# Softmax attention and a Fourier layer on one core: v loaded whole or in quarters

## The chip, the core and the metric

The kernel runs on 1 core of one Trainium2 chip. The core has five engines that each execute their own instructions in order: TensorE (PE, matmuls; its weight loads are shown as PEld), VectorE (DVE), ScalarE (ACT), GpSimd (POOL) and SyncE (SP), which here issues all DMA transfers. The time is the device time of one execution in microseconds (us); lower is better. Before the change it is 3046.23 us, the median of 3 runs (3045.86 to 3047.76).

## What is computed

Two independent layers, whose outputs stand side by side in the result. All data are 32-bit floats.

```
A:  x [1, 2048, 1024], wqkv [1024, 3072], wo [1024, 1024], 32 heads of 32 columns
    q, k, v = split(x @ wqkv)
    p = softmax(q k^T / sqrt(32))          per head, 2048 x 2048
    a = (p v, heads joined) @ wo
B:  x [1, 2048, 1024], DFT matrices of 2048 and of 1024, real and imaginary
    a = x dft_hid_re^T,  b = x dft_hid_im^T
    y = dft_seq_re a - dft_seq_im b
out = concat(A, B) in the last axis
```

## The kernel before

**Stages.** The large products (x with wqkv, the two DFT products, the projection with wo) are done in blocks with seven products in place of eight, and each 32-bit operand is split into a high and a low half, so that three matmuls (high by high, low by high, high by low) make one. These matmuls have line L356, whatever product they belong to. Their operands are loaded (L404, L413), added or subtracted (L420) and split: the high half at L442 (VectorE) or L440 (ScalarE), the low half at L445 (GpSimd or VectorE). The results of the first product, q, k and v, are stored to DRAM: `qk_d` and `v_d`. `v_d` consists of two tensors of 128 rows by 16 key tiles by 512 columns, so each holds v for 16 heads.

**Attention.** It runs head by head, with the matmuls of L356 of the other stages put between as fill. Per head there are three streams on PE:

- S, L1147: scores with the query in the rows, 128 x 1024 at a time, into one of two banks of `psS`. VectorE takes the negated row maxima (L1153), ScalarE the exponentials with the row sums (L1156), which gives the bank free.
- T, L1264: the scores transposed, 128 keys by 512 queries, into one of two banks of `psT`. The row maximum is already part of the product, by two more rows of `qs` (loaded at L1194). ScalarE writes the exponentials to one of 19 tiles `pt` (L1268).
- V, L1282: after every four key tiles (`PVB` = 4), 16 products of v with `pt` are added up in `pd`, with the four blocks of 512 queries in four column groups of the array. VectorE adds `pd` to `ot` (L1293, L1295). So a head has four groups of V, and group number t // 4 uses key tiles t-3 to t of v.

At the end `ot` is multiplied by the reciprocal row sums `rt` (loaded at L1228, four transfers) and stored (L1312).

**Loads for attention.** q and k of head h + 2 (`qs`, `ks`, L280) and v of head h + 2 (`vt`, two buffers, L1247) are asked for when head h is done with its buffers. v of a head is one transfer: 128 partitions, 16 key tiles, 32 columns, so 128 x 16 runs of 128 bytes, 256 KB.

**What sets the order.** The order of the instructions on all engines is made by a planner (class `Plan`) when the program is built. Every piece of work is an `Op` with an engine, an assumed cost, the ops that it waits for (`after`), a rank (the lowest goes first) and, for a DMA, its size `kb`. The planner goes through an assumed time. A DMA keeps SP for `ISSUE` = 0.46 us, the DMA stretch for kb / 360 us, and it has landed `LANDING` = 1.6 us later; SP begins none while more than 1 us of DMA work is outstanding or the eighth last hasn't landed. Fill is taken on PE when no stream is able, and in proportion to the progress of attention. Loads for fill have the number of finished groups as rank, the loads of attention have -2, those of L1194 -3. The real program has this order on each engine, and semaphores for the true dependences; the assumed times are not in it.

In the load of v, `vt_r.take()` returns the ops that used the buffer last (`old`) and a list for its new users; `v_st` holds the stores of `v_d`; `att_gate` what has to be done before the first buffers of attention exist:

```
vts[h] = (op("SP", ISSUE, load, old + v_st[h // 16] + (att_gate if h < 2 else []), [users], -2, 512), users)
```

The 512 is the size in KB that the planner counts, twice the real 256.

Of the kernel before, what the change touches and what calls it, by code (L numbers as in the profile page):

```python
# [8 lines left out]
F32 = mybir.dt.float32  # L9
# [7 lines left out]
P = 128  # L17
# [3 lines left out]
DH = 32  # L21
NC = D // P
NS = S // P
# [3 lines left out]
PVB = 4  # L27
# [33 lines left out]
class Plan:  # L61
# [23 lines left out]
    def op(self, engine, cost, emit, after=(), uses=(), rank=0.0, kb=0, order=None, other=None, lanes=1, two=False):  # L85

        o = Op(engine, cost, emit, rank, kb, other, two)
        o.lanes = lanes  # L90
        seen = set()
        for d in after:
            if d is not None and id(d) not in seen:
                seen.add(id(d))
                self._wait(o, d)
        for u in uses:
            u.append(o)
        if order is not None:
            p, order.first = order.first, o
            if p is not None and not p.begun:  # L100
                p.soon.append(o)
                o.left += 1
        if o.left == 0:
            self._release(o)
        return o
# [104 lines left out]
def kernel(  # L210
# [11 lines left out]
    nc = tc.nc  # L222
# [6 lines left out]
    v_d = [dram.tile([P, NS, NB], F32, name=f"v_d{b}") for b in range(2)]  # L229
# [17 lines left out]
    def f(ap):  # L247
        return ap.bitcast(F32)
# [43 lines left out]
    def att():  # L292

        if "att" not in late:
            vp.release()
            late["att"] = a = tc.alloc_tile_pool(name="att", bufs=1, reuse_waits="tile")
            QS.append(a.tile([98, S], F32R, name="qs1"))
            KS.append(a.tile([98, S], F32R, name="ks1"))
            nc.gpsimd.memset(f(KS[1])[96:98, :], 1.0)
        return late["att"]  # L300
# [3 lines left out]
    MM, PV, SWITCH, TINY = 0.234, 0.762, 0.62, 0.17  # L304
# [3 lines left out]
    ISSUE = 0.46  # L308
# [16 lines left out]
    op = pl.op  # L325
# [204 lines left out]
    v_st = [[], []]  # L530
    att_gate = []
# [586 lines left out]
    def load_qk_op(h, which, j, after):  # L1118
        g = h // 4
        got[h, which, j] = op("SP", ISSUE, lambda: load_qk(h, which, j), [*qk_st[2 * g + which][j], *after], [], -2, 192)  # L1120
# [118 lines left out]
    VT = {}  # L1239
    vts = {}  # L1240

    def load_v(h):
        old, users = vt_r.take()

        def load():
            VT[h] = att().tile([P, NS, DH], F32, name="vt", bufs=2)
            nc.sync.dma_start(VT[h], v_d[h // 16][:, :, h % 16 * DH : h % 16 * DH + DH])  # L1247

        vts[h] = (op("SP", ISSUE, load, old + v_st[h // 16] + (att_gate if h < 2 else []), [users], -2, 512), users)

    def transposed(h):
        moved = mine[h][4]
        todo = []
        po = {}
        oold, ouse = ot_r.take()
        for t in range(NS):
            for j in range(4):
                old, users = psT_r.take()
                pold, puse = pt_r.take()
                box = {}  # L1260

                def mm(t=t, j=j, box=box):
                    box["p"] = psT.tile([P, NB], F32, name="psT")
                    nc.tensor.matmul(box["p"], KS[h % 2][0:98, t * P : t * P + P], QS[h % 2][0:98, j * NB : j * NB + NB], start=True, stop=True)  # L1264

                def ex(box=box):
                    box["t"] = att().tile([P, NB], F32, name="pt", bufs=NPT)
                    nc.scalar.activation(box["t"], box["p"], AF.Exp)  # L1268

                a = op("PE", MM, mm, [*old, *moved, *(att_gate if h == t == j == 0 else []), *(got.get((h, w, k)) for w, k in ((0, j), (1, t // 4)))], [users])  # L1270
                e = op("ACT", ET, ex, [a, *pold], [users, puse], 0, 0, pt_r)
                exp_of[a] = e
                streams["T"].append((a, h, 4 * t + j))
                Tops.setdefault(h, []).append(a)
                todo.append((t, j, box, e, puse))
            if (t + 1) % PVB == 0:
                load, vuse = vts[h]

                def pv(todo=todo, t=t):
                    po["p"] = psD.tile([P, NB], F32, name="pd")  # L1280
                    for k, j, box, _, _ in todo:
                        nc.tensor.matmul(  # L1282
                            po["p"][j * DH : j * DH + DH, :], VT[h][:, k, :], box["t"], start=(k == t + 1 - PVB), stop=(k == t),
                            tile_position=(0, j * DH),
                        )

                v = op("PE", SWITCH + PVB * PV, pv, [load, *(x[3] for x in todo)], [vuse, *(x[4] for x in todo)])
                todo = []

                def gather_o(t=t):  # L1290
                    if t + 1 == PVB:
                        po["o"] = att().tile([P, NB], F32, name="ot", bufs=2)
                        nc.vector.tensor_copy(po["o"], po["p"])  # L1293
                    else:
                        nc.vector.tensor_tensor(out=po["o"], in0=po["o"], in1=po["p"], op=ALU.add)  # L1295

                e = op("DVE", EVAC, gather_o, [v] + (oold if t + 1 == PVB else []), [ouse], -1)
                streams["V"].append((v, h, e))
            if t % 4 == 3 and h + 2 < H:
                load_qk_op(h + 2, 1, t // 4, [Tops[h][-1], Sops[h][-1]])  # L1300
        if h + 2 < H:
            for j in range(4):
                load_qk_op(h + 2, 0, j, [Tops[h][-1], Sops[h][-1]])
            load_v(h + 2)
        return e, po, ouse
# [12 lines left out]
    for w in (1, 0):  # L1318
        for j in range(4):
            load_qk_op(1, w, j, att_gate)  # L1320
    load_v(0)
    load_v(1)
    scores(0)
    for h in range(H):
        if h + 1 < H:
            scores(h + 1)
        else:
            sums(h)
        result(h, *transposed(h))
# [11 lines left out]
    while nf < len(fills) or any(place[n] < len(s) for n, s in streams.items()):  # L1341
# [71 lines left out]
        t = min(times)  # L1413
# [3 lines left out]
    while True:  # L1417
        pl.others()
        t = pl.next_time()
# [31 lines left out]
```

## Time and profile before

| | |
|---|---|
| median of 3 runs | 3046.23 us |
| the profiled execution, its own time | 3044.43 us |
| its span, first to last instruction | 3042.6 us |
| mean TensorE clock granted | 0.998 |
| loads of v (L1247) | 32, first 217.8, last 2654.8 us |
| products of v (L1282) | 270.1 to 2808.2 us, first and last start |
| DMA | 557.53 MB, 183 GB/s on average |

A row of the timeline has the start and the length in us, the engine (SPq is SyncE's queue of DMA issues), the line, the operation, output and input by the program's names, the number of instructions, and in brackets how long the engine had been idle and what ended that. A row of the waits has the engine and line that waited, what for, the total in us, how often, and the longest. A matmul's duration reaches into the next one's, since they are pipelined. Buffer numbers are left out of names. Lines are those of the kernel before; in the changed kernel the lines behind `load_v` stand 6 further down.

### The profile page before, as it was taken

What the parts mean: (1) busy time and instruction counts of PE and PEld (TensorE: products, weight loads), DVE (VectorE), ACT (ScalarE), POOL (GpSimd) and SP (SyncE); (2) the same over time, 40 slices, a digit from 0 to 9 for tenths busy, and PEclk for the clock granted to TensorE, in tenths of its full rate; (3) what the DMA queues carried; (4) which work ended last, traced back from release to release, by engine and by line L of the source; (5) the groups of instructions that cost most, each with busy time, mean ns of one, the idle gap of its engine ahead of it and who ended that gap; (6) DMA issues with size and microseconds to landing.
All of it is one profiled execution on the core that took longest, in us unless ns stands there. A gap on an engine that the chain in (4) does not pass through costs nothing.

```text
span 3042.6 us, 45257 instructions
## 1 busy us (share of the span) xinstructions
PE 3009.5 (99%) x14912; PEld 2145.0 (70%) x14912; DVE 2434.8 (80%) x3284; ACT 2298.1 (76%) x4328; POOL 812.6 (27%) x606
## 2 busy tenths in 40 slices
PE   8999999999999999999999999999999999999999
PEld 7887666676676666667766666666677666666887
DVE  7779888778878887787778888888787788887886
ACT  4347888888888888888888888888888788874321
POOL 2313334222412321220111344232111234331232
PEclk9999999999999999999999999999999999999999
DMA  9975567656735544463434675545433567546942
GB/s 336 348 234 186 187 188 234 216 199 227 232 97 175 174 122 157 147 191 113 149 114 129 201 229 185 149 151 182 128 115 100 147 207 237 168 133 222 376 148 98
DMA packets 374777, 557.53 MB, mean 183 GB/s; under 512 B 109424, under 2 KB 109424, under 8 KB 374544
## 3 DMA queue, kind: packets, MB, share of 16 engines
q1 hardware_dynamic: 374544, 554.64, 56.9%
q8 instruction: 120, 1.97, 0.3%
q14 instruction: 113, 0.93, 0.1%
HBM read 401.41 MB, written 152.57 MB: 182 GB/s over the span
## 4 chain that ended last, share of the span: by engine, by line
PE 89%; DVE 5%; DMA 3%; issue 1%; ACT 1%; SPq 0%; POOL 0%; ACTq 0%; DVEq 0%; POOLq 0%
PE pd L356 38%; PE psT L1264 15%; PE psS L1147 15%; PE pd L1282 14%; PE psT L356 7%; DVE negm L1153 2%; ACT psS L1156 1%; DVE slot L442 0%; DVE h L442 0%; DMA raw<-in_wd 0%; DMA raw<-in_ct 0%; DVE raw L420 0%; DMA qk_d<-e 0%; DMA raw<-in_xa 0%; DVE slot L445 0%
## 5 line engine op out<-in xcount | busy, mean ns | idle before, releaser
L1268 ACT ACTIVATE pt<-psT 128x512 f32<-128x512 f32 x2048 | 1169.0, 638 | 350.4 <-PE psT L1264 336.6
L1153 DVE TENSOR_REDUCE negm<-psS 128x1 f32<-128x1024 f32 x1024 | 1237.7, 1220 | 192.5 <-PE psS L1147 187.0
L1156 ACT ACTIVATE psS<-psS,negm 128x1024 f32<-128x1024 f32 x1024 | 1159.8, 1133 | 91.1 <-DVE negm L1153 87.0
L356 PE MATMUL pd<-slot,h 128*128 128x512 f32 x3304 | 1135.6, 394 | 0.0
L1264 PE MATMUL psT<-qs,ks 98*128 98x512 f32 x2048 | 819.3, 403 | 0.8 <-ACT pt L1268 0.8
L356 PEld LDWEIGHTS pd<-slot,h 128*128 128x128 f32 x3304 | 625.2, 189 | 142.5 <-issue 3.4
L356 PE MATMUL pd<-slot,l 128*128 128x512 f32 x1652 | 651.2, 394 | 0.0
L1264 PEld LDWEIGHTS psT<-qs,ks 98*128 98x128 f32 x2048 | 384.2, 189 | 202.3 <-issue 84.7
L1147 PE MATMUL psS<-ks,qs 96*128 96x512 f32 x1552 | 478.2, 397 | 17.6 <-ACT psS L1156 14.5
L1282 PE MATMUL pd<-pt,vt 128*32 128x512 f32 x4096 | 467.5, 597 | 1.5 <-DVE e L641 1.2
L445 POOL TENSOR_TENSOR l<-raw,h 128x512 fp32r<-128x512 f32 x160 | 214.3, 1340 | 944.7 <-DVE h L442 335.0
L420 POOL TENSOR_TENSOR raw<-raw,g 128x512 f32<-128x512 f32 x197 | 260.2, 1325 | 486.4 <-DMA raw<-in_ct 69.8
L356 PEld LDWEIGHTS pd<-slot,l 128*128 128x128 f32 x1652 | 312.9, 189 | 70.0 <-issue 0.8
L1147 PEld LDWEIGHTS psS<-ks,qs 96*128 96x128 f32 x1552 | 290.2, 189 | 92.7 <-ACT psS L1156 27.5
L1282 PEld LDWEIGHTS pd<-pt,vt 128*32 128x32 f32 x4096 | 120.2, 110 | 277.0 <-issue 256.6
L445 POOL TENSOR_TENSOR slot<-raw,slot 128x512 fp32r<-128x512 f32 x135 | 190.7, 1420 | 389.3 <-DVE slot L442 277.5
L1156 ACT ACTIVATION_READ_ACCUMULATOR psS<-psS,negm 128x1 f32 x1024 | 256.6, 251 | 0.0
L1295 DVE TENSOR_TENSOR ot<-ot,pd 128x512 f32<-128x512 f32 x96 | 65.9, 687 | 166.9 <-PE pd L1282 166.9
L356 PE MATMUL pd<-slot,slot 128*128 128x512 f32 x768 | 194.4, 392 | 0.0
L356 PEld LDWEIGHTS pd<-slot,slot 128*128 128x128 f32 x768 | 144.3, 188 | 32.2 <-DVE slot L442 0.3
L1147 PE MATMUL psS<-ks,qx 96*128 96x512 f32 x496 | 151.8, 397 | 2.8 <-ACT psS L1156 2.5
L442 DVE CAST h<-raw 128x512 fp32r<-128x512 f32 x305 | 141.9, 467 | 13.7 <-PE pd L356 12.0
(117 smaller groups left out, 1986.5 us busy)
## 6 DMA issues: line engine op xcount, KB each, us to landing
raw<-in_ct SPq DMA_DIRECT2D x224, 256.0 KB
g<-in_ct SPq DMA_DIRECT2D x128, 256.0 KB
qk_d<-e SPq DMA_DIRECT2D x52, 512.0 KB
qs<-qk_d SPq DMA_DIRECT2D x128, 192.0 KB
ks<-qk_d SPq DMA_DIRECT2D x128, 192.0 KB
raw<-ab_d SPq DMA_DIRECT2D x96, 256.0 KB
c<-u_d SPq DMA_DIRECT2D x88, 256.0 KB
g<-ab_d SPq DMA_DIRECT2D x80, 256.0 KB
```

Of the source, the lines that this page charges most:

```text
L356: nc.tensor.matmul(box["ps"], a[1]((a[0].hi, a[0].lo)[u]()), b[1]((b[0].hi, b[0].lo)[v]()), start=k == 0, stop=k == n - 1)
L420: (nc.gpsimd if e == "POOL" else nc.vector).tensor_tensor(out=dest(), in0=dest() if a is None else a.get(), in1=other["q"] if "q" in other ...
L442: nc.vector.tensor_copy(hi(), raw())
L445: (nc.gpsimd if e == "POOL" else nc.vector).tensor_tensor(out=lo(), in0=raw(), in1=f(hi()), op=ALU.subtract)
L1147: nc.tensor.matmul(p[:, i * NB : i * NB + NB], (qx["t"] if own else QS[h % 2][0:96])[:, qt * P : qt * P + P], KS[h % 2][0:96, c * 1024 + i ...
L1153: nc.vector.tensor_reduce(out=ST["negm"][:, c, qt : qt + 1], in_=box["p"], axis=AX.X, op=ALU.max, negate=True)
L1156: nc.scalar.activation(box["p"], box["p"], AF.Exp, bias=ST["negm"][:, c, qt : qt + 1], accum_out=ST["sums"][:, c, qt : qt + 1])
L1264: nc.tensor.matmul(box["p"], KS[h % 2][0:98, t * P : t * P + P], QS[h % 2][0:98, j * NB : j * NB + NB], start=True, stop=True)
L1268: nc.scalar.activation(box["t"], box["p"], AF.Exp)
L1282: nc.tensor.matmul(po["p"][j * DH : j * DH + DH, :], VT[h][:, k, :], box["t"], start=(k == t + 1 - PVB), stop=(k == t), tile_position=(0, ...
L1295: nc.vector.tensor_tensor(out=po["o"], in0=po["o"], in1=po["p"], op=ALU.add)
```

## The change

`load_v` makes four ops of 128 KB by the planner's count in place of one of 512. Each loads four of the 16 key tiles, so a quarter of the head's v, into its part of the same tile. The first is the one that waits for the buffer and for the stores; each other one has the quarter ahead of it in its `after`, so for the planner it can begin when that one has landed. Their ranks are -2, -1, 0 and 1. A group of V has in its `after` only the quarter that it uses.

```diff
     def load_v(h):
         old, users = vt_r.take()
 
-        def load():
-            VT[h] = att().tile([P, NS, DH], F32, name="vt", bufs=2)
-            nc.sync.dma_start(VT[h], v_d[h // 16][:, :, h % 16 * DH : h % 16 * DH + DH])
-
-        vts[h] = (op("SP", ISSUE, load, old + v_st[h // 16] + (att_gate if h < 2 else []), [users], -2, 512), users)
+        def load(k):
+            if k == 0:
+                VT[h] = att().tile([P, NS, DH], F32, name="vt", bufs=2)
+            nc.sync.dma_start(VT[h][:, 4 * k : 4 * k + 4], v_d[h // 16][:, 4 * k : 4 * k + 4, h % 16 * DH : h % 16 * DH + DH])
+
+        last = old + v_st[h // 16] + (att_gate if h < 2 else [])
+        made = []
+        for k in range(4):
+            last = [op("SP", ISSUE, lambda k=k: load(k), last, [users], -2 + k, 128)]
+            made += last
+        vts[h] = (made, users)
 
     def transposed(h):
...
-                v = op("PE", SWITCH + PVB * PV, pv, [load, *(x[3] for x in todo)], [vuse, *(x[4] for x in todo)])
+                v = op("PE", SWITCH + PVB * PV, pv, [load[t // PVB], *(x[3] for x in todo)], [vuse, *(x[4] for x in todo)])
```

In the built program 128 transfers of v take the place of 32. SP keeps its other transfers, and the planner's order differs on every engine from the first load of v on.

## Prediction

> **What bounds the kernel now.** The page comes first: busy times, then the chain of work that ended last.
>
> ```profile
> span 3042.6 us, 45257 instructions
> PE 3009.5 (99%) x14912; PEld 2145.0 (70%) x14912; DVE 2434.8 (80%) x3284; ACT 2298.1 (76%) x4328; POOL 812.6 (27%) x606
> ...
> PE 89%; DVE 5%; DMA 3%; issue 1%; ACT 1%; SPq 0%; POOL 0%; ACTq 0%; DVEq 0%; POOLq 0%
> ```
>
> TensorE is busy for 3009.5 of 3042.6 us, so 33.1 us is all that a change of waits alone can win. The diff leaves the number of matmuls alone. The next view, the busy time by stretches, shows where those 33.1 us lie; its columns are the stretch, its length, then the busy time of PE, PEld, DVE, ACT and POOL, TensorE's clock, DMA share and GB/s.
>
> ```profile
> 200.00:300.00 100.00, 99.95 (x464) 76.11 (x463) 92.73 (x125) 74.86 (x136) 32.52 (x24) 1.00 0.60 186
> 300.00:2400.00 2100.00, 2088.29 (x10616) 1448.61 (x10615) 1688.28 (x2262) 1789.80 (x3403) 535.41 (x401) 1.00 0.53 165
> 2400.00:2700.00 300.00, 291.70 (x1452) 200.75 (x1452) 245.27 (x320) 243.78 (x461) 114.59 (x87) 0.99 0.62 192
> 2700.00:2850.00 150.00, 149.92 (x744) 108.47 (x743) 117.86 (x192) 67.70 (x127) 27.02 (x20) 1.00 0.71 236
> ```
>
> From 200 to 2850 us, the part in which attention runs, PE is idle for 0.05 + 11.71 + 8.30 + 0.08 = 20.1 us; 8.3 of them fall in 300 us near its end. The other 13 us are before attention or behind it, where no v transfer is issued. The waits of PE name the partner:
>
> ```profile
> PE psS L1147 <- ACT psS L1156: 17.0, 19, 4.0
> PE psT L356 <- ACT slot L440: 6.1, 1, 6.1
> ```
>
> The score matmuls of L1147 wait 19 times, 17.0 us in all, for ScalarE to release a bank of psS. The 6.1 us are the start of the program. So the question is what makes those 19 waits, and whether a load of v stands behind them. The longest, read across SP, VectorE and TensorE in the timeline (start, length, engine, instruction, and in brackets the idle time before it):
>
> ```profile
> 2400.97 0.58 SPq L1247 DMA_DIRECT2D vt<-v_d  x1
> 2401.60 4.43 SPq L413 DMA_DIRECT2D g<-ab_d  x1
> ...
> 2409.45 0.45 SPq L404 DMA_DIRECT2D raw<-ab_d  x1
> 2416.91 0.69 DVE L420 TENSOR_TENSOR raw<-raw,g 128x512 f32<-128x512 f32 x1 [5.29 <-DMA raw<-ab_d]
> 2420.08 0.73 PE L1147 MATMUL psS<-ks,qs 96*128 96x512 f32 x2 [4.04 <-ACT psS L1156]
> 2421.62 5.14 PE L1282 MATMUL pd<-pt,vt 128*32 128x512 f32 x32
> ```
>
> The load of v is issued in 0.58 us, but the issue behind it takes 4.43 us. A load further back lands late, an addition waits for it at the head of VectorE's queue for 5.29 us, the maxima behind it are late, ScalarE's exponentials too, and PE stands for 4.04 us. Here the load of v is in front of the late load. At the next long wait it isn't:
>
> ```profile
> 2570.10 0.50 SPq L404 DMA_DIRECT2D raw<-in_ct  x1
> 2571.97 0.57 SPq L1247 DMA_DIRECT2D vt<-v_d  x1
> 2575.17 1.29 POOL L420 TENSOR_TENSOR raw<-raw,g 128x512 f32<-128x512 f32 x1 [11.23 <-DMA raw<-in_ct]
> 2576.49 1.76 DVE L420 TENSOR_TENSOR raw<-raw,g 128x512 f32<-128x512 f32 x1 [3.37 <-POOL raw L420]
> 2580.74 0.73 PE L1147 MATMUL psS<-ks,qs 96*128 96x512 f32 x2 [2.67 <-ACT psS L1156]
> ```
>
> The late raw<-in_ct was issued 1.87 us ahead of v. What made it late stands in front of it; cutting v cannot bring it forward.
>
> **What v costs the queue.** The first two loads of v stand back to back:
>
> ```profile
> L1247 SPq DMA_DIRECT2D vt<-v_d x32: 570/576/3867, 217.8 to 2654.8; - x32
> 217.77 4.54 SPq L1247 DMA_DIRECT2D vt<-v_d  x2
> 222.36 1.15 SPq L1132 DMA_DIRECT2D qx<-qk_d  x1
> ```
>
> The second needs 3.867 us to issue, against a median of 0.576: SP stands until the pieces of the first (128 partitions by 16 tiles, 2048 runs of 128 B) have mostly gone out. So one load of v occupies the queue for about 4 us, for 256 KB. A quarter, 512 runs, should hold it about 1.0 us. That is an estimate, 3.87 / 4; its ends are the issue of a 64 KB transfer, 0.46 us (below), if nothing is held, and 3.87 us if the hold doesn't shrink with the size.
>
> **The wait that the change adds.** In the built program no quarter waits on the semaphore of the quarter ahead. SP waits only for the transfer eight issues back, as for every DMA. The planner's clock places the quarters: 1 to 8 issues apart, usually with the store of o and the four loads of rt between the first two. So no new wait is put on SP, and what follows SP in its queue is held by shorter pieces.
>
> **Is v itself late?** The load for head 2 and its first use:
>
> ```profile
> 335.43 0.58 SPq L1247 DMA_DIRECT2D vt<-v_d  x1
> 431.48 3.64 PE L1282 MATMUL pd<-pt,vt 128*32 128x512 f32 x32
> ```
>
> It is 96 us ahead. In the new order at most 19 issues lie between a first and a last quarter; between the second head's first quarter and the last head's there are 1915 issues over some 2437 us (217.8 to 2654.8), 1.27 us each, so 24 us. The cover is 96 us, the cost nothing; without it PE would stand for up to 24 us a head.
>
> **More issues on SP.** 96 more. The nearest rows: four 64 KB loads of rt in 1.85 us, 0.46 us each; and v's own 0.576, which has the same nesting.
>
> ```profile
> 2576.68 1.85 SPq L1228 DMA_DIRECT2D rt<-r_d  x4
> SPq L866 <- DVE e L859: 249.2, 82, 8.7
> ```
>
> So 32 x (4 x 0.46 - 0.576) = +40 us to 96 x 0.576 = +55 us on SP. They are hidden in SP's own waits: one group of stores alone waits 249.2 us for VectorE. I take 0 for PE. Where SP has no such wait, a load is 0.5 us later per quarter in front of it, less than the hold it saves.
>
> The Trainium skill, "DMA: Bandwidth & Descriptors", section "Anatomy of one DMA — SWDGE (gpsimd) path", speaks against the change: every DMA has a fixed cost of about 2.0 us whatever its size, so 96 more would be an estimated 192 us if they stood one behind another. The four rt issues in 1.85 us do not agree with a fixed cost that is served one by one. The sum does not use it.
>
> **PE's own work.** The order of PE differs from the first loads of v on, since the planner places everything after them anew. All counts of matmuls are equal. A score matmul follows a transposed one 137 times, formerly 143; at a whole matmul each that is at most 6 x 0.403 = 2.4 us either way, and I take 0. Groups of L1282 that wait for a load beside VectorE, and so need a separate wait, go from 4 to 28:
>
> ```profile
> L1264 PE MATMUL psT<-qs,ks 98*128 98x512 f32 x2048 | 819.3, 403 | 0.8 <-ACT pt L1268 0.8
> L1282 PEldq EVENT_SEMAPHORE  x4: 51/51/51, 269.7 to 1464.4; - x4
> ```
>
> 24 x 0.051 = 1.2 us if none is covered, 0 if the load has long landed; I take 0, as it has. VectorE receives 9 instructions more, since more subtractions (L445) and fewer additions (L420) go to it from GpSimd: 9 x 0.69 us (the addition above) = 6.2 us, inside VectorE's idle fifth of the span.
>
> **The clock behind a stall.** The group of L1282 right after the 4.04 us stall took 5.14 us, against 3.64 at 431.48: 1.5 us more. The clock, the third column from the end, shows why:
>
> ```profile
> 1766.11 0.58 SPq L1247 DMA_DIRECT2D vt<-v_d  x1
> 1776.04 0.73 PE L1147 MATMUL psS<-ks,qs 96*128 96x512 f32 x2 [1.35 <-ACT psS L1156]
> 1777.00:1778.00 1.00, 1.00 (x6) 0.82 (x5) 1.00 (x1) 1.00 (x3) 0.90 (x1) 1.00 0.85 240
> ...
> 2422.00:2423.00 1.00, 1.00 (x8) 0.20 (x4) 1.00 (x2) 1.00 (x4) 0.43 (x1) 0.50 0.89 260
> 2583.00:2584.00 1.00, 1.00 (x3) 0.74 (x3) 0.31 (x1) 1.00 (x3) 0.77 (x1) 0.50 1.09 350
> ```
>
> The clock fell to 0.50 after the stalls of 4.04 and 2.67 us and stayed at 1.00 after one of 1.35 us. A long stall therefore costs its length and about 1.5 us more. The Trainium skill, "TensorE: Matmul & The Clock Gate", in "Part 1: The HAM clock gate (the "warmup" mystery)", puts the drop behind an idle window of some 3.4 us; here 2.67 us were enough. By that rule a stall cut to 2 us would keep its clock, and the sum below would be 1.5 us lower.
>
> **The sum.** At 2401 us, of the 4 us that v takes, two quarters would by the usual spacing still be ahead of raw<-ab_d, so it lands 2.0 us earlier, and the stall goes from 4.04 to 2.0 us. A 2.0 us stall is nearer to 2.67 than to 1.35, so I let the slow clock stay. That is -2.0 us, with ends of 0 (the quarters bunch up) and -5.5 (4.04 + 1.5, the stall goes altogether). Everything else is 0. 3044.43 us, the profiled execution's own time, of which 3042.6 are span, becomes 3042.4. The median of the runs is 3046.23, 1.8 more than that execution, so the forecast is 3044.2 us. What this can't fix is the placing of all later waits anew: the stretches show 0.56 us idle per 100 us from 300 to 2400, and 2.77 in the next 300. With PE 99% busy, the same work in another order can win at most the 20.1 us and can lose more.
>
> **Rivals.** *All long stalls go.* If the 2.67 us stall, too, belongs to the bunch of loads at a head's boundary, and spreading v loosens it: (4.04 + 1.5) + (2.67 + 1.5) + 1.35 = 11.1 us less, 3035. For it: all three follow a load of v by 9 to 19 us. Against it: raw<-in_ct was issued ahead of v.
>
> *Slower: each quarter holds the queue almost as a whole load does.* Place: loads issued between the first and the last quarter, up to 24 us behind a head's boundary, which now have three further holds in front of them. Price: a boundary like the one at 2401 us costs 4.04 + 1.5 = 5.5 us; two more are +11 us, 3057. It decides where a quarter holds SP for more than about 1.3 us, a third of 3.87, as then three of them exceed what v held before. Against it: the rt row. For it: late loads of 1 to 5 us do reach PE. The fixed cost that the skill's page on DMA names would work in this direction.
>
> *Slower by the new order.* The planner doesn't know the 4 us (it counts 512 KB at 360 per us, 1.4 us), so stalls fall where they fall; two more stretches of 300 us like the one from 2400, at 8.30 us instead of 1.67, are +13 us, 3059.
>
> *Nothing is done:* the planned spacing doesn't hold on the chip, the quarters go out together and hold SP for 4 us as before: 3046.
>
> **How the numbers follow.** Forecast 0.46, all long stalls go 0.17, quarters hold the queue 0.22, a worse order 0.12, nothing done 0.03. A difference of 0.2%, 6.1 us, is about what a measurement of this kernel can tell from no change. The forecast's own range is 3037 to 3051: of its 0.46, 0.13 lie below 3040.1 and 0.03 above 3052.3. Faster is 0.13 + 0.15 = 0.28; slower 0.03 + 0.19 + 0.12 = 0.34; the rest, 0.38, is within. The range reaches to the three rivals, 3034 to 3059.
>
> **What would show it.** Right: SP's issue behind each quarter takes at most 1.5 us, and no issue of 3 to 4 us stands behind v; PE's waits of L1147 for ScalarE sum to 12 to 18 us; no PE wait names vt. Wrong: a quarter followed by an issue of over 2 us; PE's idle time from 200 to 2850 us above 30 us or below 10; or VectorE's waits for a load just behind the third or fourth quarter.

## The result and the profile after

The changed kernel takes 3037.26 us, the median of 20 runs (3030.75 to 3046.0), against 3044.77 us for 20 runs of the kernel before taken beside them (3039.68 to 3049.16). The ratio is 0.9978, with an interval of 0.997 to 0.9985: 0.0022 x 3044.77 = 6.7 us less, between 4.6 and 9.1. The ratio compares all the runs and is not the quotient of the two medians, which are 7.5 us apart. The kernel is faster by about what such a measurement can just tell from no change, and the gain is three times the 2.0 us that was forecast. The time lies at the lower edge of the forecast's own range, 3037 to 3051 us, and the prediction had put only 0.13 of its 0.46 on times below 3040.1.

The profiled execution took 3040.01 us. Its page, span and busy time:

```profile
span 3038.2 us, 45363 instructions
...
PE 3008.3 (99%) x14912; PEld 2144.6 (71%) x14912; DVE 2436.4 (80%) x3293; ACT 2298.6 (76%) x4328; POOL 805.0 (26%) x597
```

TensorE (PE) sets the end as before, with 29.9 us idle for 33.1. That difference, 3.2 us, has to be looked at by stretches before it is believed. The busy time by stretches, with the columns of the prediction (stretch, length, busy time of PE, PEld, DVE, ACT, POOL, clock, DMA share, GB/s), first of the kernel before for the stretch that the prediction didn't show, then of the changed kernel:

```profile
0.00:200.00 200.00, 191.07 (x821) 156.94 (x822) 142.16 (x194) 76.49 (x128) 45.21 (x37) 0.99 0.91 323
```

```profile
0.00:200.00 200.00, 193.78 (x840) 158.49 (x841) 141.32 (x199) 79.93 (x132) 46.13 (x38) 1.00 0.92 328
200.00:300.00 100.00, 98.64 (x454) 74.49 (x454) 89.36 (x119) 76.27 (x141) 35.88 (x27) 1.00 0.57 177
300.00:2400.00 2100.00, 2090.88 (x10631) 1453.76 (x10630) 1698.66 (x2275) 1790.28 (x3405) 526.57 (x393) 1.00 0.53 166
2400.00:2700.00 300.00, 294.21 (x1472) 202.43 (x1471) 255.67 (x330) 248.05 (x471) 111.55 (x84) 1.00 0.62 191
2700.00:2850.00 150.00, 146.57 (x718) 104.99 (x718) 110.34 (x187) 61.35 (x113) 29.09 (x21) 0.99 0.74 250
```

Three things are to be seen. Up to 200 us no v is loaded and both kernels do the same, yet the one is idle 8.93 us and the other 6.22: two executions differ there by accident (three of the kernel before, in the table below, differ as much). In 2400 to 2700 the idle time falls from 8.30 to 5.79 us. And two stretches that were almost free of idle time have some: 1.36 us in 200 to 300, 3.43 us in 2700 to 2850. Idle time from 200 to 2850 us is 1.36 + 9.12 + 5.79 + 3.43 = 19.7 us, against 20.1, so one trace of each hardly shows a gain. The rest is in the clock and in what differs from one execution to the next. So the comparisons by stretch below use this sum: PE's idle time, plus its busy time times the part of the clock that was missing, added up over windows of 1 us. For 2400 to 2700 it is 8.30 + 3.4 = 11.7 us before and 5.79 + 0.0 = 5.8 us after.

| us lost by idle time and slow clock | 0-200 | 200-300 | 300-2400 | 2400-2700 | 2700-2850 |
|---|---|---|---|---|---|
| before | 10.6 | 0.1 | 11.7 | 11.7 | 0.1 |
| before_2 | 6.7 | 0.1 | 10.6 | 17.5 | 0.0 |
| before_3 | 8.2 | 0.1 | 12.8 | 18.4 | 0.0 |
| after | 6.2 | 1.4 | 10.8 | 5.8 | 5.0 |
| again | 6.8 | 1.4 | 11.4 | 3.0 | 4.4 |
| new_order_whole | 6.2 | 1.4 | 8.2 | 10.3 | 4.4 |
| old_order_in_a_row | 7.3 | 0.1 | 10.4 | 10.0 | 0.4 |
| old_order_spaced | 7.5 | 0.1 | 12.1 | 6.0 | 0.0 |
| old_order_spaced_2 | 8.1 | 0.1 | 9.5 | 4.9 | 0.2 |
| old_order_long_runs | 10.7 | 0.1 | 10.2 | 6.2 | 0.4 |
| old_order_long_runs_2 | 5.9 | 0.1 | 11.3 | 6.8 | 0.0 |
| whole_planned_256 | 7.2 | 1.4 | 15.3 | 8.1 | 2.9 |
| whole_planned_1440 | 6.4 | 1.7 | 11.0 | 1.2 | 4.4 |
| quarters_planned_360 | 7.7 | 1.4 | 9.7 | 1.9 | 2.7 |

(The other names are the experiments below; before_2 and before_3 are two more executions of the kernel before, again one of the changed kernel.) The sums from 200 us on say where the time went. From 2400 to 2700, the mean of three executions before is 15.9 us and of two after 4.4: -11.5 us. From 300 to 2400 it is 11.7 against 11.1: -0.6. The two stretches in the new order cost +1.3 and +4.7. That is -6.1 us, against the 6.7 measured. The agreement is closer than so few traces warrant: from 2400 to 2700 those of the kernel before alone range from 11.7 to 18.4.

The place where the prediction put its gain, in the changed kernel's timeline (start, length, engine, instruction, and in brackets the idle time before it):

```profile
2395.02 0.38 SPq L1248 DMA_DIRECT2D vt<-v_d  x1
2395.60 0.49 SPq L413 DMA_DIRECT2D g<-ab_d  x1
...
2396.78 3.33 SPq L1228 DMA_DIRECT2D rt<-r_d  x4
2400.47 0.38 SPq L1248 DMA_DIRECT2D vt<-v_d  x1
...
2402.13 0.32 SPq L404 DMA_DIRECT2D raw<-ab_d  x1
2402.50 0.43 SPq L1248 DMA_DIRECT2D vt<-v_d  x1
2403.52 0.43 SPq L1248 DMA_DIRECT2D vt<-v_d  x1
2407.96 0.69 DVE L420 TENSOR_TENSOR raw<-raw,g 128x512 f32<-128x512 f32 x1 [2.02 <-DMA raw<-in_ct]
2411.14 0.74 PE L1147 MATMUL psS<-ks,qs 96*128 96x512 f32 x2 [0.76 <-ACT psS L1156]
...
2570.55 0.74 PE L1147 MATMUL psS<-ks,qs 96*128 96x512 f32 x2 [1.59 <-ACT psS L1156]
```

And the same addition in a second execution of the changed kernel (again, below):

```profile
2408.83 0.69 DVE L420 TENSOR_TENSOR raw<-raw,g 128x512 f32<-128x512 f32 x1 [1.26 <-DMA raw<-ab_d]
```

The issue right behind the first quarter takes 0.49 us where it took 4.43. Two quarters stand ahead of raw<-ab_d, as predicted; the other two are behind it. VectorE waits 2.02 us instead of 5.29, and PE 0.76 instead of 4.04. The row puts that wait down to raw<-in_ct, a load issued right behind the fourth quarter, but it is the same load as before, raw<-ab_d: its last part landed at 2407.86, while parts of raw<-in_ct still landed after the addition had begun, and the second execution names raw<-ab_d. The four loads of rt, though, take 3.33 us from the first to the last, where the prediction's row for four such had 1.85. That is not v's hold in another place: with v in long runs (below) they take 3.01 us. Three of the four now wait, 1.7 us in all, for the transfer eight issues back to land, which in the kernel before has landed by the time that SP gets there. The stall that stood at 2580 is 1.59 us. The waits of PE (engine and line that waited, for what, us in total, times, longest):

```profile
PE psS L1147 <- ACT psS L1156: 11.5, 18, 1.7
...
PE psT L356 <- DVE l L445: 2.6, 2, 2.4
PE psT L1270 <- ACT pt L1274: 2.1, 3, 0.8
```

The waits for ScalarE at L1147 fell from 17.0 to 11.5 us, the longest from 4.0 to 1.7. The other two rows had 0.3 and 0.8 us before. What is new in them, in the timeline:

```profile
247.06 0.50 PE L1270 MATMUL psT<-qs,ks 98*128 98x512 f32 x1 [0.69 <-ACT pt L1274]
249.83 0.50 PE L1270 MATMUL psT<-qs,ks 98*128 98x512 f32 x1 [0.64 <-ACT pt L1274]
...
2825.96 0.42 DVE L442 CAST h<-raw 128x512 fp32r<-128x512 f32 x1
2826.29 0.68 DVE L859 TENSOR_TENSOR e<-slot,pd 128x512 f32<-128x512 f32 x1
2827.01 1.05 DVE L864 TENSOR_TENSOR e<-c,e 128x512 f32<-128x512 f32 x1
2827.98 0.68 DVE L420 TENSOR_TENSOR raw<-raw,g 128x512 f32<-128x512 f32 x1
2828.58 0.68 DVE L445 TENSOR_TENSOR l<-raw,h 128x512 fp32r<-128x512 f32 x1
...
2829.32 0.80 PE L356 MATMUL psT<-slot,l 128*128 128x512 f32 x1 [2.38 <-DVE l L445]
```

The two halves of the same operand in the kernel before:

```profile
2833.81 0.76 DVE L442 CAST h<-raw 128x512 fp32r<-128x512 f32 x2
2834.48 0.68 DVE L445 TENSOR_TENSOR l<-raw,h 128x512 fp32r<-128x512 f32 x1
```

At 2829 no load is late. In VectorE's new order three other element-wise operations stand between the high half h and the low half l of one operand, 2.2 us from the end of the cast to the start of the subtraction, where before the subtraction came right behind the cast. PE's next matmul needs l. It waits 2.38 us, and the clock is 0.50 in the two windows of 1 us behind it; the stretch loses 5.0 us in all.

### The profile page after: what moved, and what is told of

It reads as the page before. It is cut to its first block, busy times and chain, and to the rows that moved or that the text cites. A ratio compares the mean times of both kernels' runs of the same rounds, so it can differ in the third digit from the quotient of the medians.

```text
span 3038.2 us, 45363 instructions
## 1 busy us (share of the span) xinstructions
PE 3008.3 (99%) x14912; PEld 2144.6 (71%) x14912; DVE 2436.4 (80%) x3293; ACT 2298.6 (76%) x4328; POOL 805.0 (26%) x597
## 4 chain that ended last, share of the span: by engine, by line
PE 73%; DVE 4%; DMA 2%; ACT 1%; issue 1%; SPq 0%; POOL 0%; ACTq 0%; DVEq 0%; POOLq 0%
PE pd L356 32%; PE psT L1270 13%; PE pd L1288 13%; PE psS L1147 12%; PE psT L356 3%; DVE negm L1153 2%; ACT psS L1156 1%; DVE raw L420 1%; DMA raw<-in_ct 0%; DVE h L442 0%; DMA raw<-ab_d 0%; DMA g<-s_d 0%; DVE l L445 0%; SPq L280 0%; DMA o_d<-ot 0%
## 5 line engine op out<-in xcount | busy, mean ns | idle before, releaser
L1147 PE MATMUL psS<-ks,qs 96*128 96x512 f32 x1552 | 476.8, 396 | 8.8 <-ACT psS L1156 7.4
L420 POOL TENSOR_TENSOR raw<-raw,g 128x512 f32<-128x512 f32 x207 | 274.8, 1334 | 495.8 <-DMA raw<-in_ct 91.0
L445 POOL TENSOR_TENSOR l<-raw,h 128x512 fp32r<-128x512 f32 x141 | 190.3, 1350 | 762.5 <-PE psT L1270 307.0
L1147 PEld LDWEIGHTS psS<-ks,qs 96*128 96x128 f32 x1552 | 290.5, 189 | 82.6 <-ACT psS L1156 19.1
L1147 PE MATMUL psS<-ks,qx 96*128 96x512 f32 x496 | 151.9, 397 | 4.1 <-ACT psS L1156 4.1
L442 DVE CAST h<-raw 128x512 fp32r<-128x512 f32 x305 | 139.4, 458 | 15.2 <-PE pd L356 14.1
```

The lines of the kernel that those rows point to most:

```text
L420: (nc.gpsimd if e == "POOL" else nc.vector).tensor_tensor(out=dest(), in0=dest() if a is None else a.get(), in1=other["q"] if "q" in other ...
L442: nc.vector.tensor_copy(hi(), raw())
L445: (nc.gpsimd if e == "POOL" else nc.vector).tensor_tensor(out=lo(), in0=raw(), in1=f(hi()), op=ALU.subtract)
L1147: nc.tensor.matmul(p[:, i * NB : i * NB + NB], (qx["t"] if own else QS[h % 2][0:96])[:, qt * P : qt * P + P], KS[h % 2][0:96, c * 1024 + i ...
```

## The experiments

Two theories were put against each other. Theory 1: the gain comes from the queue, since a piece of v holds SP's next issues for less long. Theory 2: it comes from the new order that the planner made when it had four loads to place. The kernels of the first batch have each half of the change by itself. Their line numbers differ by up to 10 where lines were added.

**again**: the changed kernel once more.

> The changed kernel once more, beside the three others on the same chip. Both theories: 0.997 to 0.9985 of the kernel before, as measured. It is the measure for the others.

Measured: 0.9984 (0.9975 to 0.9993), median 3040.3 of 11 runs. The waits at L1147 are 9.4 us, the stretches are those of after: nothing of 0.5 us or more at 2400, 3.0 us lost in 2400 to 2700, 4.4 in 2700 to 2850. The small gain repeats, and so do both new losses.

**new_order_whole**: the changed kernel's order with all of v in one transfer, at the place of the first quarter.

```diff
             if k == 0:
                 VT[h] = att().tile([P, NS, DH], F32, name="vt", bufs=2)
-            nc.sync.dma_start(VT[h][:, 4 * k : 4 * k + 4], v_d[h // 16][:, 4 * k : 4 * k + 4, h % 16 * DH : h % 16 * DH + DH])
+                nc.sync.dma_start(VT[h], v_d[h // 16][:, :, h % 16 * DH : h % 16 * DH + DH])
```

> The planner plans four quarters, as in the changed kernel, so the order on PE, VectorE, ScalarE and GpSimd is that of the changed kernel; but the whole of v is loaded in one transfer at the first quarter's place, and the other three places are empty. Theory 1 (shorter holds of the queue save the time): the holds of 3 to 4 us behind v are back, and the ratio to the kernel before is 0.9995 to 1.003. Theory 2 (the new order saves it, the size of the transfers nothing): 0.997 to 0.9985, with PE's waits of L1147 for ScalarE near 11.5 us as in the changed kernel.

Measured: 0.9996 (0.9985 to 1.0006), no difference that can be told. From its timeline:

```profile
2390.86 0.57 SPq L1248 DMA_DIRECT2D vt<-v_d  x1
2391.49 4.02 SPq L413 DMA_DIRECT2D g<-ab_d  x1
...
2408.29 0.73 PE L1147 MATMUL psS<-ks,qs 96*128 96x512 f32 x2 [2.33 <-ACT psS L1156]
...
2828.34 0.50 PE L356 MATMUL psT<-slot,l 128*128 128x512 f32 x1 [2.49 <-DVE l L445]
```

The 4 us hold behind v and the stall at 2400 are back, and the stall at 2829 is there without any quarters. Theory 2 falls: in sum the order alone wins nothing (the 10.3 us lost in 2400 to 2700 are fewer than before, but the two new losses take that back), and the loss at 2829 belongs to the order.

**old_order_in_a_row**: the order before, with four quarters issued one right after another.

```diff
-            nc.sync.dma_start(VT[h], v_d[h // 16][:, :, h % 16 * DH : h % 16 * DH + DH])
+            for k in range(4):
+                nc.sync.dma_start(VT[h][:, 4 * k : 4 * k + 4], v_d[h // 16][:, 4 * k : 4 * k + 4, h % 16 * DH : h % 16 * DH + DH])
```

> The order of the kernel before on every engine; in place of one transfer of v, its four quarters are issued one behind another. Theory 1: the queue is held for about 4 us as before, so 0.9990 to 1.0015. Theory 2: the order is the old one, 0.9990 to 1.0010. Both expect no change; a gain would mean that small transfers help by themselves, a loss over 0.2% that three more issues cost.

Measured: 0.9968 (0.9956 to 0.9981). The expectation missed: pieces in a row were to hold the queue as the whole does. From its timeline:

```profile
2393.78 3.57 SPq L1248 DMA_DIRECT2D vt<-v_d  x4
2397.40 1.52 SPq L413 DMA_DIRECT2D g<-ab_d  x1
...
2408.03 0.69 DVE L420 TENSOR_TENSOR raw<-raw,g 128x512 f32<-128x512 f32 x1 [3.33 <-DMA raw<-ab_d]
2411.21 1.22 PE L1147 MATMUL psS<-ks,qs 96*128 96x512 f32 x2 [2.06 <-ACT psS L1156]
```

The four issues and the one behind take 3.57 + 1.52 = 5.1 us, as 0.58 + 4.43 = 5.0 did, so SP is held as long. But VectorE's wait is 3.33 us instead of 5.29, and the addition begins 14.25 us after the first issue of v (2408.03 - 2393.78), against 15.94, 15.86 and 16.34 in the three executions before: 1.8 us less in the same order. That this comes from cutting the transfer is not shown by these times, since new_order_whole, with one whole transfer, has 14.25 us too (2390.86 to 2405.11), and whole_planned_256 14.70. The gain in the ratio stands; through which wait it comes is open.

**old_order_spaced**: the order before, with the second, third and fourth quarter slipped in 5, 10 and 13 of SP's issues behind the first, about as the changed kernel spaces them.

```diff
-            nc.sync.dma_start(VT[h], v_d[h // 16][:, :, h % 16 * DH : h % 16 * DH + DH])
+            quarter(h, 0)
+            pl.later += [None] * 5 + [lambda: quarter(h, 1)] + [None] * 4 + [lambda: quarter(h, 2)] + [None] * 2 + [lambda: quarter(h, 3)]
+
+        def quarter(h, k):
+            nc.sync.dma_start(VT[h][:, 4 * k : 4 * k + 4], v_d[h // 16][:, 4 * k : 4 * k + 4, h % 16 * DH : h % 16 * DH + DH])
```

> The order of the kernel before on PE, VectorE, ScalarE and GpSimd; on SP the first quarter takes the place of v and the other three are slipped in 5, 10 and 13 issues later, as the changed kernel has them on average. Theory 1: the stall of 4.04 us at 2420 us goes to about 2 us or goes altogether, and the ratio is 0.9975 to 0.999. Theory 2: 0.9995 to 1.0010, the stalls stay where they were.

Measured: 0.9946 (0.9932 to 0.9959), median 3030.55 of 5 runs. It beats both kernels, and by more than was expected. From its timeline:

```profile
2395.00 0.38 SPq L1257 DMA_DIRECT2D vt<-v_d  x1
2395.44 0.66 SPq L419 DMA_DIRECT2D g<-ab_d  x1
...
2407.25 0.69 DVE L426 TENSOR_TENSOR raw<-raw,g 128x512 f32<-128x512 f32 x1 [1.29 <-DMA raw<-ab_d]
...
2569.48 0.73 PE L1153 MATMUL psS<-ks,qs 96*128 96x512 f32 x2 [2.81 <-ACT psS L1162]
```

The same load has 12.25 us to the addition (11.92 in a second execution), VectorE waits 1.29 us, and PE has no stall of 0.5 us or more there. The stall near 2570, whose late load goes out ahead of v, stays at 2.81 us here. And the two losses of the new order aren't there (0.1 us lost in 200 to 300, 0.0 in 2700 to 2850). This is the gain of the quarters without the price of the order.

**old_order_long_runs**: the order before, one transfer of 256 KB, but read as 128 runs of 2 KB instead of 2048 of 128 bytes. The values are other columns of v than the head's.

```diff
-            nc.sync.dma_start(VT[h], v_d[h // 16][:, :, h % 16 * DH : h % 16 * DH + DH])
+            nc.sync.dma_start(VT[h].rearrange("p s d -> p (s d)"), v_d[h // 16][:, h % 16, :])
```

> The order of the kernel before on every engine, v in one transfer; but each partition takes 2 KB in one run from the stored v (256 KB as before, 128 runs in place of 2048), which are other values than the head's v. Theory 1 (the hold of the queue by 2048 short runs costs the time): no issue behind v over 1 us, and at least the gain of the spaced quarters in the old order: 0.993 to 0.996. Theory 3 (the gain of the old-order kernels has another source than the hold, for instance how early the rest of the program begins): 0.998 to 1.001.

Measured: 0.9979 (0.9969 to 0.999), less than expected. From its timeline:

```profile
217.87 0.89 SPq L1247 DMA_DIRECT2D vt<-v_d  x2
...
2399.19 0.38 SPq L1247 DMA_DIRECT2D vt<-v_d  x1
...
2410.16 0.69 DVE L420 TENSOR_TENSOR raw<-raw,g 128x512 f32<-128x512 f32 x1 [0.26 <-DMA raw<-ab_d]
```

Two loads of v in a row take 0.89 us instead of 4.54, nothing is held behind one, the addition begins 10.97 us after the issue, and neither stall at 2400 nor the one at 2511 (below) is there. So the hold is a matter of the many short runs, not of the 256 KB. The ratio lies between the ranges of the two theories that the expectation names, 0.0001 below that of theory 3, by which the gain has another source than the hold. The trace speaks for theory 1 at 2400; the time of the whole does not decide. This trace also gives the zero for the others: against 10.97 and, in a second execution, 11.15 (11.1), a whole v in the old order costs the load behind it 16.0 - 11.1 = 4.9 us, four quarters in a row 14.25 - 11.1 = 3.2, and two spaced quarters 12.25 - 11.1 = 1.1. Only a part of the 4.9 us is SP's: raw<-ab_d goes out 8.5 to 9.0 us behind v in the three executions before, and 6.8 and 7.0 us behind it with long runs. The rest arises between its issue and the landing of its last part, 6.8 to 7.6 us before and 4.1 to 4.2 with long runs.

**whole_planned_256, whole_planned_1440, quarters_planned_360**: only the size that the planner counts is changed, and with it the order. 256 is the real size of v in KB. 1440 KB at its 360 KB per us is 4.0 us, near the measured hold of a whole load, and 360 KB is 1.0 us, near that of a quarter.

```diff
-        vts[h] = (op("SP", ISSUE, load, old + v_st[h // 16] + (att_gate if h < 2 else []), [users], -2, 512), users)
+        vts[h] = (op("SP", ISSUE, load, old + v_st[h // 16] + (att_gate if h < 2 else []), [users], -2, 1440), users)
```

```diff
-            last = [op("SP", ISSUE, lambda k=k: load(k), last, [users], -2 + k, 128)]
+            last = [op("SP", ISSUE, lambda k=k: load(k), last, [users], -2 + k, 360)]
```

> One transfer of v, as before, but counted with 256 KB by the planner in place of 512: the plan is made anew, with nothing about v changed on the chip. It shows how far a new plan alone moves the time. Theory 1 with a new order that costs or gains by chance: anywhere from 0.997 to 1.004. Theory 2 (planning four quarters makes a better order): 1.000 to 1.002, since nothing is better planned here.

> One transfer of v, counted with 1440 KB, which is 4.0 us by the planner's 360 KB per us, as long as the trace shows it to hold the queue. Theory 1: the hold stays, but loads behind it are planned later; 0.996 to 1.001. If what matters is only that the planner knows the hold, as much as the spaced quarters gain: 0.994 to 0.997.

> The changed kernel with each quarter counted with 360 KB, 1.0 us, in place of 128. Theory 1: shorter holds and a planner that knows them: 0.994 to 0.998, better than the changed kernel unless its new order is unlucky. Theory 2: like the changed kernel, 0.997 to 0.9985.

Measured: 0.9995 (0.9985 to 1.0004), 0.9971 (0.9961 to 0.9982) and 0.9959 (0.9945 to 0.9972). The stretch from 2400 in whole_planned_1440:

```profile
2400.00:2700.00 300.00, 298.77 (x1517) 206.91 (x1516) 254.04 (x342) 242.89 (x464) 111.55 (x82) 1.00 0.61 196
```

PE is idle 1.23 us there, and 1.86 in quarters_planned_360, against 8.30, and in the first of the two v is still one transfer, with issues of up to 3.9 us behind it. That fits a planner that brings other loads forward once it counts what a load really holds; but each size has given one order only, and whether the count or chance made these two good is not shown. By the expectations, whole_planned_256 lies in the wide range that chance was given, whole_planned_1440 in the range for a hold that stays and just outside that for a planner that knows it, and quarters_planned_360 in that of theory 1. Both still pay 4.4 and 2.7 us in 2700 to 2850: every order that was made anew has the stall of 2.4 to 2.5 us for VectorE's l there, and none with the order before.

**before_2, before_3, old_order_spaced_2, old_order_long_runs_2**: no edit; second and third traces, to see what one trace of the kernel before hides, and whether long runs and spaced quarters lose alike.

> The kernel before again, for a second trace. In the first 200 us the program is the same in all kernels, yet the traces of the kernel before and of the long runs lose 10.6 us there (idle and slow clock), the others 6.2 to 7.7. If that is an accident of one execution: 6 to 11 us here, at random. If it belongs to the program: 10 to 11 us. The stalls at 2420 us (about 4 us) and near 2580 us (about 2.7 us) come back in either case.

> As before_2, a third trace: accident 6 to 11 us in the first 200 us, program 10 to 11 us.

> The spaced quarters in the old order again. Accident: 6 to 11 us lost in the first 200 us; program: 7 to 8 us. The stall at 2420 us stays away in either case; the one near 2570 us comes back, with 2.5 to 3 us.

> The long runs in the old order again, with other values than the head's v in the products. Accident: 6 to 11 us lost in the first 200 us; program: 10 to 11 us. The stall at 2420 us stays away, the one near 2570 us comes back.

Measured, one time each: 3043.43, 3047.26, 3030.16 and 3032.7 us. From the timeline of before_2:

```profile
2409.96 0.69 DVE L420 TENSOR_TENSOR raw<-raw,g 128x512 f32<-128x512 f32 x1 [5.25 <-DMA raw<-ab_d]
2413.14 1.22 PE L1147 MATMUL psS<-ks,qs 96*128 96x512 f32 x2 [3.99 <-ACT psS L1156]
...
2486.90 0.57 SPq L1247 DMA_DIRECT2D vt<-v_d  x1
2487.83 2.31 SPq L1312 DMA_DIRECT2D o_d<-ot  x1
...
2510.96 0.73 PE L1147 MATMUL psS<-ks,qs 96*128 96x512 f32 x2 [2.03 <-ACT psS L1156]
```

The stall at 2400 repeats in each trace (4.04, 3.99, 4.47 us). But behind the next head's v there is a second one, 2.03 us here and 2.19 in before_3, which the trace that the prediction was made from hasn't got. It is gone in the traces of spaced quarters and of long runs. The three traces before lose 11.7, 17.5 and 18.4 us in 2400 to 2700, so the one that was read first was the mildest.

What stays open: spaced quarters and long runs lose alike in their traces (6.0 and 4.9 us against 6.2 and 6.8 in that stretch), and their single times of one batch are 2.5 us apart, but the compared ratios are 0.9946 and 0.9979, on two chips. Which of them is really better wasn't settled. The gains do not go by SP's hold alone: four quarters in a row, which hold SP as long as before, gain as much (0.9968) as long runs (0.9979), behind which no issue is held for more than 1.3 us. Nor does the sum by stretches reach the whole gain of old_order_spaced: from 200 us on, -10.4 in 2400 to 2700 and -0.9 in 300 to 2400 make 11.3 us, against 14.1 between the medians and 0.0054 x 3044.6 = 16.4 (12.5 to 20.7) by the ratio. And no run tells what delays the load behind v between its issue and its landing.

## Why the prediction was right, and where its size was off

**Luck.** The chain through SP, VectorE and the bank of psS was foreseen, and the time lies in the range. But it does so because two errors of opposite sign met: the gain was about 12 us instead of 2.0, and the new order, priced at 0, cost 6. With the order left alone, old_order_spaced ran in 3030.55 us, below the whole range.

**Bound.** Right: PE is 99% busy before and after, and what changed is its waits and its clock.

**What a quarter holds.** Right. The last four of six quarters in a row at the start of the changed kernel, from its timeline:

```profile
218.76 4.06 SPq L1248 DMA_DIRECT2D vt<-v_d  x4
```

That is 1.02 us each, against the estimate of 1.0; the longest single one is 1.71. The rival "each quarter holds the queue almost as a whole load does" decided at more than 1.3 us, and fell. So did "nothing is done": the spacing holds on the chip. The long issues have become fewer. Counted one by one in the two traces, 58 took over 1 us before (106 us in sum) and 45 after (60 us); right behind a transfer of v, 16 took over 2 us before and none after.

**The wait that the change adds, v itself being late, and more issues on SP.** Right at nothing: no wait of PE names vt, and old_order_spaced, with the same 96 more issues, is 0.5% faster than the kernel without them. The Trainium skill, "DMA: Bandwidth & Descriptors", "Anatomy of one DMA — SWDGE (gpsimd) path", gives its fixed 2.0 us for a DMA that GpSimd issues; taken over to SyncE's, it pointed the other way. No run here shows such a price for the 96 more transfers.

**The sum.** This is the step that failed, in size. The prediction let the load come 2.0 us earlier and the stall shrink from 4.04 to 2.0 us with its slow clock kept: -2.0 us, with -5.5 as the end "if the stall goes altogether". Two quarters were ahead of raw<-ab_d, as said. But a whole v had cost that load 4.9 us, not 4, and two quarters cost about 1, not 2.0. The prediction counted the time on SP's queue alone. On it the load goes out 7.1 and 7.2 us behind v instead of 8.5 to 9.0, so less than the 2.0 us is won there; as much again is won between its issue and its landing, 5.7 and 4.9 us instead of 6.8 to 7.6, for which the sum had no term. So the addition waits some 3 to 4 us less, and the stall went to 0.76 us in one execution and below 0.5 in the other, and its slow clock with it. The second term missing is the stall behind the next head's v, which the single trace didn't have. Together with the stall at 2580 they make -11.5 us in 2400 to 2700. That is nearly the price of the rival "all long stalls go", 11.1 us, though its parts are others.

**The stall at 2580.** "Cutting v cannot bring it forward" is not settled. In the order before the stall is 2.67, 2.98 and 3.25 us with whole loads and 2.52 and 3.25 with long runs, which speaks for it; but it is 2.81 and 1.54 with spaced quarters and 1.48 with four in a row. In the changed kernel it is 1.59 us and absent in the second execution, in new_order_whole 1.78, so the new order has a part in it.

**The placing anew.** Priced at 0, with a rival of +13 us by two more bad stretches. It cost about +6 us in the changed kernel, 1.3 at 247 and 4.7 at 2829. Both stalls are in every order made anew, and in none with the order before. The rival was right in its kind and about half its size, but its mechanism wasn't late loads: it was VectorE's order, with three other operations ahead of an operand that PE needs next. This takes back half of the gain, and is the whole reason why the changed kernel is behind old_order_spaced, as far as the stretches show it.

**The clock.** The prediction let a stall of 2.0 us keep its slow clock. The drop turned out not to be fixed by the length, see below.

**What would show it.** PE's idle time from 200 to 2850 us, 19.7, lies between the bounds named, and of the 128 issues behind a quarter two are over 1.5 us (1.71 and 1.59), none over 2. The waits at L1147, 11.5 and 9.4 us, are below the 12 to 18 stated, which is the same error as in the sum. The third sign of being wrong seems to show, as the row at 2407.96 names a load right behind the fourth quarter; but that load isn't the one waited for, as said above.

## What to carry to other kernels

A transfer of many short runs holds the queue for far longer than its bytes say; look at the issue behind it and at when the loads further back land, and if an in-order engine stands at the end of that chain, cut the transfer or lengthen its runs. When a planner makes the order anew from a changed cost, price the new order by itself: keep the order and change the transfer, then keep the transfer and change the order, because here the first was worth up to 0.5% and the second gave half of it back. And read two or three traces of the kernel before, since one execution can lack a stall that most have.

## What was not expected of the hardware

**Short runs delay the loads behind them twice.** Against 256 KB in runs of 2 KB, the same bytes in 2048 runs of 128 bytes sent the load raw<-ab_d out 1.5 to 2.2 us later and let it take 2.6 to 3.5 us longer from issue to landing. Four transfers of 512 runs in a row sent it out as late (8.5 us), but it took 5.6 us to land instead of 6.8 to 7.6; one whole transfer in the new order had 8.1 and 6.2. So that one transfer costs more than its four parts is not shown.

**The clock doesn't go by the length of a stall alone.** The same stall of 1.70 us, in before_2, with the group of V behind it and the window of 1 us after it:

```profile
809.19 0.73 PE L1147 MATMUL psS<-ks,qx 96*128 96x512 f32 x2 [1.70 <-ACT psS L1156]
810.22 3.64 PE L1282 MATMUL pd<-pt,vt 128*32 128x512 f32 x32 [0.29 <-DVE c L589]
811.00:812.00 1.00, 1.00 (x16) 0.30 (x12) 1.00 (x3) 0.61 (x1) 0.23 (x1) 1.00 0.58 197
```

and in the changed kernel:

```profile
810.51 0.73 PE L1147 MATMUL psS<-ks,qx 96*128 96x512 f32 x2 [1.70 <-ACT psS L1156]
811.53 5.34 PE L1288 MATMUL pd<-pt,vt 128*32 128x512 f32 x32 [0.29 <-DVE c L589]
812.00:813.00 1.00, 1.00 (x12) 0.36 (x8) 1.00 (x3) 0.29 (x1) 0.00 (x0) 0.50 0.78 170
```

The clock, the third column from the end, stays at 1.00 in the one and is 0.50 in the other, and the same group of 32 matmuls takes 5.34 us instead of 3.64, 1.7 us more. In these traces the clock fell after a stall as short as 1.54 us (old_order_spaced_2, near 2566) and stayed at 1.00 after one of 2.48 us (quarters_planned_360, near 2821). Between the two it goes either way. Their clock records give each slow stretch behind a stall as 3.41 us or twice that, which is where the 1.7 us come from: half of 3.41. The Trainium skill, "TensorE: Matmul & The Clock Gate", "Part 1: The HAM clock gate (the "warmup" mystery)", puts the drop behind an idle window of some 3.4 us; that does not agree with the drop behind 1.70 us.

**The start differs by itself.** In the first 200 us, which no edit touches, 5.9 to 10.7 us are lost from one execution to another. A difference of 4 us between two single executions can be made there.
